# Turning the first two tiles by plain products with the identity in place of transposes, with two more filler products between them

## Chip, cores, metric

One core of one Trainium2 chip. The metric is device time in microseconds of one execution of the program, on its slowest (here its only) core; lower is better.

PE is TensorE, the matrix engine, PEld its loads of weights (in the products with `w1`, the pieces of `w1` are the weights), ACT ScalarE, DVE VectorE, POOL GpSimd, and SPq the queue of SyncE, which issues most transfers. PSUM is the memory that PE writes to. To "turn" a 128x128 block is to transpose it; "the head" is the first 15 us or so.

## The reference, cut to what matters

```python
x = A_x                                   # 2048 x 1024, bf16
xn = layernorm(x)
return x + state_space(xn, ...) + dense_mish(xn, w1, b1, w2)
```

The change touches only the beginning: the first 512 rows of `x` must be normalised, turned so that the 1024 features lie on partitions, and multiplied by `w1`. To start before the statistics of tiles 0 and 1 (128 rows each) are known, the kernel turns their raw `x`, multiplies by `w1`, and corrects for mean and deviation afterwards.

## The kernel before

PE first runs "fillers", products of zeros that nobody reads, to keep it busy while data come. The order of PE in the head is this (cuts marked):

```python
def first_transpose(q):
    for k in range(NK):                                   # 8 blocks of 128 x 128
        bank, d = bank_T(q, k), slice(k * P, (k + 1) * P)
        src, b_src = (xx[:, 0, q, d], b_xx[0][q]) if q < 2 else (xn[:, q, d], b_xn[q])
        PE.mm(lambda e, ...: e.transpose(ps16(bank)[:, d], src, ident[:]), ...)

def first_copy(q, queue, k0=0, k1=NK):                    # PSUM -> xr (q < 2) or xnT
    ...
    srcp = ps16(bank).rearrange("p (k t) -> p k t", k=NK)[:, k0:k1, :]
    # ScalarE copy, or VectorE tensor_copy for tile 3

keep_busy(18)                                             # fillers
first_transpose(0)
keep_busy(14)
first_transpose(1)
keep_busy(6)
# then: 257-column products (256 rows of raw x and a column of ones) with the first piece
# of w1, a spreading of the statistics by 8 small products, products with the second,
# third and fourth piece, between them the turns of tiles 2 and 3, ...
```

Later, on GpSimd, the four loads of `x` for block 1 stand between phase tables, and SP loads B by transposing transfers between the pieces of `w1`:

```python
for j in range(NJ):
    phases(j)                         # GpSimd
    if j == 3:
        for q in range(NQ):
            load_x(PO, 1, q)          # block 1's x
...
SP.dma(lambda e, ...: e.dma_start_transpose(BT[:, ci, j, :, :], src[j * P:(j + 1) * P, :]), ...)
```

## Time and profile before

| | before |
|---|---|
| time, first three runs | 620.87 us median (620.79 to 623.14) |
| span of the profiled run | 619.6 us |
| PE busy | 616.1 us, 99% |
| PE at half rate until | about 6.9 us (128-column products and transposes 103 to 107 ns apart, 56 ns after it) |
| PE's wait for the third w1 piece | 0.22 us as the profile counts it (0.38 us from start to start, see below) |
| first product of tiles 2 and 3 (L553) | 15.45 us |

PE is never short of work from 15.45 us on, so the time is that moment plus a constant, as long as nothing makes PE wait later. The lines that show this stand in the prediction.

### The profile page before, as it was taken

The page shows a single profiled execution, that of the slowest core. Times are in us where ns is not written, and L with a number is a line of the kernel's source. Part 1 is how long each engine was busy: PE and PEld are TensorE (multiplying, and loading weights), DVE is VectorE, ACT ScalarE, POOL GpSimd, SP SyncE. Part 2 cuts the span into 40 slices and gives each one's busy share as a digit, 9 for nine tenths or more (in the row PEclk, how much of TensorE's full clock was granted, in tenths as well). Part 3 has the DMA queues.
Part 4 walks back from the last instruction along what each step waited for, and adds up shares of the span by engine and source line. Part 5 has one row for each costly group of instructions (what it writes and reads, how often), then busy time and mean ns, then how long its engine had stood idle before and what let it go on. Part 6 is the DMA issues. An engine that isn't in the chain of part 4 may idle for free.

```text
span 619.6 us, 7424 instructions
## 1 busy us (share of the span) xinstructions
PE 616.1 (99%) x2957; PEld 288.4 (47%) x2957; DVE 467.3 (75%) x698; ACT 247.5 (40%) x161; POOL 53.1 (9%) x57
## 2 busy tenths in 40 slices
PE   9999999999999999999999999999999999999998
PEld 7644444444444444444444444444444444444444
DVE  6989999999467599998147659999624856999603
ACT  4589997441079940000009992000001999000000
POOL 2899100000100000000010000000000000000000
DMA  8999986840454401783054430286203542033001
GB/s 249 252 254 298 225 167 202 206 136 0 146 191 140 135 2 37 204 201 103 17 187 135 158 114 1 96 184 189 75 35 107 173 162 68 1 123 116 1 0 69
DMA packets 97917, 79.94 MB, mean 129 GB/s; under 512 B 51034, under 2 KB 80346, under 8 KB 97882
## 3 DMA queue, kind: packets, MB, share of 16 engines
q1 hardware_dynamic: 94384, 72.17, 42.3%
q10 hardware_dynamic: 2538, 4.14, 1.8%
q0 software_dynamic: 960, 3.15, 1.8%
q8 instruction: 24, 0.39, 0.3%
q14 instruction: 11, 0.09, 0.1%
HBM read 63.19 MB, written 4.19 MB: 109 GB/s over the span
## 4 chain that ended last, share of the span: by engine, by line
PE 98%; DMA 1%; SPq 1%; issue 0%; DVE 0%
PE ps L820 49%; PE ps L740 29%; PE ps L762 18%; DMA ring<-in_B_w_dram 1%; PE ps L553 1%; PE ps L544 0%; SPq L310 0%; PE ps L834 0%; PE ps L397 0%; SPq L343 0%; SPq L314 0%; DVE xx L888 0%
## 5 line engine op out<-in xcount | busy, mean ns | idle before, releaser
L820 PE MATMUL ps<-ring,act 128*128 128x512 bf16 x896 | 194.0, 379 | 0.0
L740 PE MATMUL ps<-xnT,ring 128*128 128x512 bf16 x840 | 182.0, 379 | 0.0
L718 ACT ACTIVATE act<-hb 128x3584 bf16<-128x3584 bf16 x16 | 50.9, 3183 | 220.6 <-DVE hb L749 220.4
L820 PEld LDWEIGHTS ps<-ring,act 128*128 128x128 bf16 x896 | 87.7, 98 | 105.7
L740 PEld LDWEIGHTS ps<-xnT,ring 128*128 128x128 bf16 x840 | 82.2, 98 | 98.9
L749 DVE TENSOR_SCALAR hb<-ps,par 128x512 bf16<-128x512 f32 (+1 forms) x112 | 80.0, 730 | 52.6 <-PE ps L740 51.7
L762 PE MATMUL ps<-xnT,BT 128*128 128x512 bf16 x512 | 111.2, 379 | 0.0
L820 PE MATMUL ps<-CT,hT 128*128 128x512 bf16 x506 | 109.9, 379 | 0.0
L767 DVE TENSOR_TENSOR mt<-ps,tab 128x1024 bf16<-128x1024 f32 x64 | 75.4, 1219 | 13.3 <-PE ps L762 11.7
L762 PEld LDWEIGHTS ps<-xnT,BT 128*128 128x128 bf16 x512 | 50.1, 98 | 60.4
L820 PEld LDWEIGHTS ps<-CT,hT 128*128 128x128 bf16 x506 | 49.5, 98 | 59.7
L785 DVE TENSOR_TENSOR_SCAN hT<-cs,qi,hT 128x512 bf16<-128x512 f32 x48 | 58.9, 1269 | 0.0
L865 DVE TENSOR_TENSOR xx<-ps,xx 128x1024 bf16<-128x1024 f32 (+1 forms) x16 | 18.8, 1190 | 45.1 <-PE ps L820 45.0
L720 ACT ACTIVATE act<-act 128x3584 bf16<-128x3584 bf16 x16 | 51.0, 3190 | 0.2
L719 ACT ACTIVATE act<-act 128x3584 bf16<-128x3584 bf16 x16 | 51.0, 3190 | 0.2
L790 DVE TENSOR_TENSOR mt<-hT,tab 128x1024 bf16<-128x1024 bf16 x64 | 41.4, 688 | 1.1
L725 DVE TENSOR_TENSOR act<-act,hb 128x3584 bf16<-128x3584 bf16 x16 | 33.2, 2075 | 2.3 <-ACT act L720 2.3
L310 POOL DMA_DIRECT2D xx<-in_A_x_dram x12 | 6.7, 560 | 249.4 <-DVE xx L865 245.1
L694 ACT ACTIVATE ct<-CT,cs 128x512 f32<-128x512 bf16 x16 | 11.5, 718 | 25.3 <-DVE CT L696 25.3
L719 ACT ACT_TABLE_LOAD x16 | 20.5, 1283 | 0.3
L720 ACT ACT_TABLE_LOAD x16 | 20.5, 1283 | 0.3
L785 DVE TENSOR_TENSOR_SCAN hT<-cs,hT 128x512 bf16<-128x512 f32 x16 | 18.7, 1208 | 0.0
(101 smaller groups left out, 294.1 us busy)
## 6 DMA issues: line engine op xcount, KB each, us to landing
ring<-in_B_w_dram SPq DMA_DIRECT2D x112, 512.0 KB, 4.0
out_dram<-xx ACTq DMA_DIRECT2D x15, 256.0 KB, 2.1
xx<-in_A_x_dram POOLq DMA_DIRECT2D x12, 256.0 KB, 4.3
xx<-in_A_x_dram SPq DMA_DIRECT2D x3, 256.0 KB, 4.4
xx<-in_A_x_dram SPq DMA_DIRECT2D x2, 128.0 KB, 2.3
dsk<-in_A_Dskip_dram SPq DMA_DIRECT2D x1, 256.0 KB, 7.4
xnT<-xn SPq DMA_TRANSPOSE x14, 4.6
BT<-in_A_B_re_dram SPq DMA_TRANSPOSE x8, 6.3
```

The lines of the kernel that those rows point to most:

```text
L718: aop(lambda e: e.activation(a, hs, AF.Exp), reads=[b_hb[g % 2]], writes=[b_act[g]])
L719: aop(lambda e: e.activation(a, a, AF.Ln, bias=1.0), reads=[b_act[g]], writes=[b_act[g]])
L720: aop(lambda e: e.activation(a, a, AF.Tanh), reads=[b_act[g]], writes=[b_act[g]])
L725: vop(lambda e: e.tensor_tensor(a, a, hs, op=ALU.mult), reads=[b_act[g], b_hb[g % 2]], writes=[b_act[g]])
L740: PE.mm(lambda e, k=k, w=w: e.matmul(ps[:, bank, :], lhsT=w, rhs=xnT[:, k, :], start=k == 0, stop=k == NK - 1), reads=[b_ring[s]] + b_xnT, ...
L749: vop(lambda e: e.tensor_scalar(hb[:, hs, ts], ps[:, bank, ts], b1(f), None, op0=ALU.add), reads=[b_ps[bank], b_par], writes=[b_hbf[hs]])
L762: PE.mm(lambda e, j=j, ci=ci, k=k, bank=bank: e.matmul(ps[:, bank + ci, :], lhsT=BT[:, ci, j, k, :], rhs=xnT[:, k, :], start=k == 0, stop= ...
L767: vop(lambda e, s=s, u=u, j=j: e.tensor_tensor(mt[:, s, :, :], u, tab[:, s, j, :].unsqueeze(1).to_broadcast([P, 2, TB]), op=ALU.mult), rea ...
L785: vop(lambda e, ci=ci, init=init: e.tensor_tensor_scan(out=hT[:, ci, j, :], data0=cj("r", j).to_broadcast([P, TB]), data1=hT[:, ci, j, :], ...
L790: vop(lambda e, s=s: e.tensor_tensor(mt[:, s, :, :], hT[:, :, j, :], tab[:, s, j, :].unsqueeze(1).to_broadcast([P, 2, TB]), op=ALU.mult), ...
L820: PE.mm(lambda e: e.matmul(ps[:, u, :], lhsT=lhsT, rhs=rhs, start=st_, stop=last), reads=reads, writes=[b_ps[u]], first=st_, last=last)
L865: vop(lambda e: e.tensor_tensor(xr, src, xr, op=ALU.add), reads=b_ps[bank:bank + n] + [b_x], writes=[b_x])
```

## The change

Intent: an earlier or surer full rate of PE. The change rests on an assumption of the author that transposes count less than products towards it; the trace of before didn't show it, and e1, g2 and g3 below refute it (full rate at 5.4, 5.0 and 4.6 us after transposes alone). A product with the identity gives the same turned block, but into fp32 PSUM, half a tile to a bank (128x512 f32). Two more fillers are added between the turns.

```diff
         for k in range(NK):
             bank, d = bank_T(q, k), slice(k * P, (k + 1) * P)
             ...
-            PE.mm(lambda e, ...: e.transpose(ps16(bank)[:, d], src, ident[:]),
+            o = (k % (NK // 2)) * P
+            put = (lambda e, ...: e.matmul(
+                ps[:, bank, o:o + P], lhsT=src, rhs=ident[:], start=True, stop=True)) if q < 2 else (
+                lambda e, ...: e.transpose(ps16(bank)[:, d], src, ident[:]))
+            PE.mm(put, ...
...
-        srcp = ps16(bank).rearrange("p (k t) -> p k t", k=NK)[:, k0:k1, :]
+        srcp = (ps[:, bank, :].rearrange("p (k t) -> p k t", k=NK // 2) if q < 2 else
+                ps16(bank).rearrange("p (k t) -> p k t", k=NK)[:, k0:k1, :])
...
     first_transpose(0)
-    keep_busy(14)
+    keep_busy(16)
     first_transpose(1)
```

In the changed file the lines are five lower: L506 becomes L511, L544 L549, L553 L558, L740 L745, L762 L767; the turns at L397 become L399 (products) and L401 (transposes of tiles 2 and 3).

More of the change, by code (lines that the diff above doesn't have):

```diff
@@ L396, in first_transpose @@
             src, b_src = (xx[:, 0, q, d], b_xx[0][q]) if q < 2 else (xn[:, q, d], b_xn[q])
-            PE.mm(lambda e, bank=bank, d=d, src=src: e.transpose(ps16(bank)[:, d], src, ident[:]),
-                  reads=[b_src.parts[k // (NK // 2)], b_ident], writes=[b_ps[bank]],
+            o = (k % (NK // 2)) * P
+            put = (lambda e, bank=bank, o=o, src=src: e.matmul(
+                ps[:, bank, o:o + P], lhsT=src, rhs=ident[:], start=True, stop=True)) if q < 2 else (
+                lambda e, bank=bank, d=d, src=src: e.transpose(ps16(bank)[:, d], src, ident[:]))
+            PE.mm(put, reads=[b_src.parts[k // (NK // 2)], b_ident], writes=[b_ps[bank]],
                   first=k == 0 or bank != bank_T(q, k - 1), last=k == NK - 1 or bank != bank_T(q, k + 1))
```

## The prediction

Passages that rested on what no trace of this case shows are cut from the prediction, with the cuts marked. The forecast's sum came to 0.0 us for an ordinary run, within 0.1 either way: cost 0.0 at an unchanged clock, gain 0.0 at an earlier one. The steps from "Then sixteen fillers" on suppose one. The 620.3 to 621.7 us rest on the rivals.

> **What bounds the kernel now.** I began with the page: PE is busy 616.1 of 619.6 us, so only time in which PE stands still, or repeats work at a lower clock, can be won. Then I read the chain that ended last in order of time, to see whether the edited part, the first 7 us, is on it (start us, length us, what):
>
> ```profile
> 4.24 7.49 DMA ring<-in_B_w_dram
> 11.73 0.05 issue
> 11.78 1.07 PE ps L544 x8
> 12.84 0.45 PE ps L397 x8
> ...
> 616.14 1.32 PE ps L834 x12
> 617.46 0.02 issue
> 617.49 0.42 DVE xx L888
> ```
>
> From 11.78 us to the end the chain is PE work without a gap (the cut lines are all PE). Before it stands one transfer, the third piece of w1, issued at 4.24 and landed at 11.73; ahead of that are only the SP queue's issues. None of the turning at 3 to 6.5 us is on the chain. The waits of PE in the first 40 us say the same (waited for: us, times, longest):
>
> ```profile
> PE ps L506 <- DVE filler L353: 1.0, 1, 1.0
> PE ps L544 <- DMA ring<-in_B_w_dram: 0.2, 1, 0.2
> ```
>
> PE is idle for 0.22 us before 11.78, because of that transfer. So the head has 0.22 us to spare: what makes it earlier only lengthens this wait, and what makes it later by less than that costs nothing.
>
> Next I read PE's row by row order in the head, for the clock (start, busy, instructions):
>
> ```profile
> 1.04 2.10 PE L506 MATMUL ps<-filler 128*128 128x128 bf16 x18 [1.04 <-DVE filler L353]
> 3.20 1.03 PE L397 MATMUL ps<-ident,xx 128*128 128x128 bf16 x8
> 4.03 1.70 PE L506 MATMUL ps<-filler 128*128 128x128 bf16 x14
> 5.52 1.06 PE L397 MATMUL ps<-ident,xx 128*128 128x128 bf16 x8
> 6.37 0.82 PE L506 MATMUL ps<-filler 128*128 128x128 bf16 x6
> 7.01 1.97 PE L544 MATMUL ps<-xr,ring 128*128 128x257 bf16 x16
> 9.59 1.96 PE L544 MATMUL ps<-xr,ring 128*128 128x257 bf16 x16
> 11.78 1.07 PE L544 MATMUL ps<-xr,ring 128*128 128x257 bf16 x8 [0.22 <-DMA ring<-in_B_w_dram]
> 12.68 0.61 PE L397 MATMUL ps<-ident,xn 128*128 128x128 bf16 x8
> ```
>
> A row holds the spacing of its instructions plus the length of the last one. With the lengths of the groups below (314 ns cold, 219 warm): fillers (2.10-0.31)/17 = 105 ns and (1.70-0.31)/13 = 107 ns; turns (1.03-0.31)/7 = 103 and (1.06-0.31)/7 = 107 ns; the later turns of tile 2 (0.61-0.22)/7 = 56 ns. The 257-column products at 7.01 are (1.97-0.27)/15 = 113 ns apart, as those at 11.78 are ((1.07-0.27)/7 = 114). So PE runs at half rate until about 7.0 us, six microseconds after its first filler, and at full rate after. The column of granted clock says 1.00 throughout and doesn't show this; the durations do:
>
> ```profile
> L506 PE MATMUL ps<-filler 128*128 128x128 bf16 x38 | 4.6, 313 | 1.0 <-DVE filler L353 1.0
> L407 ACT COPY xr<-ps 128x512 bf16<-128x512 bf16 x4 | 2.1, 589 | 0.9 <-PE ps L397 0.9
> L397 PE MATMUL ps<-ident,xx 128*128 128x128 bf16 x16 | 2.1, 312 | 0.1
> L397 PE MATMUL ps<-ident,xn 128*128 128x128 bf16 x16 | 1.2, 219 | 0.0
> L435 ACT COPY yz<-ps 128x512 f32<-128x512 f32 x1 | 0.6, 585 | 0.4 <-PE ps L431 0.4
> ```
>
> [...]the trace shows filler products and transposes at the same 103 to 107 ns, so nothing is lost on PE.[...] The copies agree: 589 ns from bf16 PSUM, 585 ns from fp32.
>
> **The change part by part.** Sixteen transposes become sixteen plain products of the same shape: 16 x about 105 ns before and after at the same clock, difference 0.[...] The banks stay (6 and 4 for tile 0, 7 and 5 for tile 1), half a tile per bank, so no new bank dependence. Four ScalarE copies now read fp32: 4 x (585-589) ns, nothing. Two more fillers: 2 x 106 = 0.21 us if cold, 2 x 56 = 0.11 us if warm.
>
> At an unchanged clock all that follows tile 1's turn shifts by 0.21 us. The first sixteen products then run from 7.22 to about 9.0; the eight spreading products, which started at 9.04 after GpSimd's split (8.30+0.30 = 8.60), start about 0.1 to 0.2 later; the next sixteen end at 11.7 instead of 11.56 (11.78-0.22). The transfer lands at 11.73. Cost: 0.0 us.
>
> [...]Then sixteen fillers take 0.9 us in place of fourteen in 1.5, tile 1 is turned at about 5.0 (its data must have landed) in 0.45 in place of 0.85, six fillers take 0.34, and the sixteen products can start at about 6.0, one microsecond sooner. The spreading still needs the split: GpSimd waited 5.1 us for VectorE's rr, and VectorE's statistics run back to back from 5.03 to 6.5 whatever PE does; at best rr comes 0.1 us sooner. So PE stands still for about a microsecond before the spreading, the second sixteen start at about 9.5, end at about 11.45, and the wait for the transfer is 0.3 us in place of 0.22. Gain: 0.0 us. The transfers can't come sooner: SP issues all nine from 0.79 to 5.25 without waiting for an engine, and the transposing transfers after them hang on VectorE's xn at 7.5, not on PE.
>
> Sum for an ordinary run: 0.0 us, within 0.1 either way.
>
> [...]
>
> **The rivals.** (1) An earlier clock shortens the run, by up to the 0.85+1.7+0.6 us that the cold head wastes. For it: half rate until 7 us. Against: the wait for the transfer at 11.73, with no PE work before it on the chain. It would need an earlier landing; then 619 to 620 us. (2) The extra fillers, or slower fp32 reads, push PE past 11.73: 0.22 us of slack against 0.21, and 585 against 589 ns; at worst 621.0.[...] (4) The 623-us runs come from late transfers and not from the clock; then they stay, and a median of three can land on one.
>
> **Range and chances.** The ordinary run gives 620.8. Below, only rival 1 leads, and the transfer stands against it: 620.3. Above are rivals 2 and 4[...]: 621.7. A change of 2% would be 12.4 us, more than the whole head lasts before the transfer lands, so nothing here reaches it.
>
> **What would show it.** Right: the chain after still begins with the transfer of w1 landing near 11.7 and PE L544 straight after; PE's wait for it is 0.1 to 0.5 us; the turns of tile 1 are 56 ns apart with lengths of about 219 (the clock came early) or[...] still 107; the copies stay at 585 to 590 ns; the spread of runs is narrower. Wrong: the chain leads back through PE or ScalarE before 11.7, the transfer lands at another time, or the products at 9.6 are more than 114 ns apart.

## The result and the profile after

Ratios are the mean time of one kernel's fast runs over that of the other's of the same rounds, so not quite the ratio of the medians. In the first comparison the change took 621.13 us (median of 6, 620.27 to 623.69) and before 621.46 (6 runs, 620.79 to 623.14): ratio 0.9994, interval 0.9970 to 1.0017. In a second comparison (f4 below) it took 621.96 against 620.53, ratio 1.0020, interval 0.9995 to 1.0045. No difference is shown in either direction, and both kernels scatter by some 4 us.

The profiled run of the change was its slowest, 623.69 us (span 622.4), so I read it for what is common to all runs first. PE in the head, in order of time (start, busy, instructions):

```profile
3.20 1.03 PE L399 MATMUL ps<-ident,xx 128*128 128x128 bf16 x8
4.02 1.91 PE L511 MATMUL ps<-filler 128*128 128x128 bf16 x16
5.73 1.06 PE L399 MATMUL ps<-ident,xx 128*128 128x128 bf16 x8
6.58 0.68 PE L511 MATMUL ps<-filler 128*128 128x128 bf16 x6
7.13 1.95 PE L549 MATMUL ps<-xr,ring 128*128 128x257 bf16 x16
10.31 3.17 PE L549 MATMUL ps<-xr,ring 128*128 128x257 bf16 x24 [0.55 <-DMA ring<-in_B_w_dram]
```

The turns take 1.03 and 1.06 us as products, exactly what they took as transposes in before. The fillers' row grew from 1.70 to 1.91 us, the predicted 0.21. The clock is no earlier: the last half-rate product starts at 6.8 us. ScalarE's copies of the turned halves cost what they did, 589 ns from fp32 as from bf16 in before (group: busy, mean ns):

```profile
L412 ACT CAST xr<-ps 128x512 bf16<-128x512 f32 x4 | 2.2, 589 | 1.2 <-PE ps L399 1.2
```

What is new in this run is outside the edited lines. PE's longest wait over the whole span (us in total, times, longest), and the two rows of VectorE that explain it:

```profile
PE ps L767 <- DVE hb L754: 1.8, 1, 1.8
...
```

```profile
47.41 1.43 DVE L449 BATCH_NORM_STATS2 stats<-xx 128x6 f32<-128x512 bf16 x2 [2.51 <-DMA xx<-in_A_x_dram]
...
51.12 1.42 DVE L449 BATCH_NORM_STATS2 stats<-xx 128x6 f32<-128x512 bf16 x2 [0.78 <-DMA xx<-in_A_x_dram]
```

VectorE stood waiting for block 1's `x` until 47.41 us (45.72 in the trace of before) and again until 51.12. The work behind it in program order, the emptying of PSUM banks (L754), came late, and PE stood still for 1.8 us near 62 us, waiting for VectorE. In the head, PE waited for the second piece of w1, until 10.31, and then for the third. The third is missing from PE's list of waits: of the 0.41 us between the starts of the two products, where 0.11 is normal, the first counts as busy for 0.27, and the 0.14 left are too short for that list. The loads of weights show both waits:

```profile
10.30 1.68 PEld L549 LDWEIGHTS ps<-xr,ring 128*128 128x128 bf16 x16 [0.72 <-DMA ring<-in_B_w_dram]
12.40 0.79 PEld L549 LDWEIGHTS ps<-xr,ring 128*128 128x128 bf16 x8 [0.42 <-DMA ring<-in_B_w_dram]
```

So this run is slow by late transfers.

### Where the time goes in every trace

The traces of all fourteen profiled runs add up the same way. "Half rate until" is the start of the last product or transpose with a half-rate duration (the change to full rate after it is called the release below); then come the landing of the third piece of w1, the start of the first product that reads it, and that of the first product of tiles 2 and 3. "Stands still after" sums the gaps between starts of PE's products after that, less the normal spacing (gaps of twice the spacing that recur every 10.8 us are taken for missing records and left out).

| trace | what it is | half rate until | third piece lands | product on it | tiles 2, 3 at | stands still after | run, us |
|---|---|---|---|---|---|---|---|
| before | | 6.9 | 11.73 | 11.78 | 15.45 | 0 | 620.88 |
| after | the change | 6.8 | 12.36 | 12.41 | 16.11 | 2.1 | 623.69 |
| e1 | all turns and fillers transposes | 5.4 | 11.72 | 11.77 | 15.44 | 0 | 620.88 |
| g2 | as e1 | 5.0 | 11.27 | 11.32 | 15.07 | 0.45 | 620.98 |
| g3 | as e1 | 4.6 | 12.08 | 12.12 | 15.85 | 0.46 | 621.76 |
| e2 | the change, 14 fillers | 6.7 | 11.40 | 11.45 | 15.20 | 0.9 | 621.60 |
| e3 | before, 26 fillers | 6.9 | 11.53 | 12.25 | 15.88 | 2.1 | 623.31 |
| e4 | the change, block 1's x early | 6.4 | 11.42 | 11.47 | 15.22 | 0 | 620.57 |
| f1 | before, no fillers | 12.0 | 11.84 | 13.98 | 17.61 | 0 | 622.97 |
| f2 | before, block 1's x early | 6.3 | 12.63 | 12.67 | 16.40 | 2.3 | 624.17 |
| f3 | as e4 | 5.7 | 12.01 | 12.06 | 15.76 | 0 | 621.11 |
| f4 | the change | 5.6 | 12.18 | 12.22 | 15.95 | 2.1 | 623.42 |
| g1 | the change, B loaded plainly | 6.0 | 12.02 | 12.07 | 15.75 | 0 | 621.10 |
| h1 | the change | 4.1 | 11.77 | 11.82 | 15.50 | 1.9 | 622.74 |

Take "tiles 2, 3 at" and "stands still after" from the span, and 604.1 us remain in each, within 0.1. (The time of a run is some 1.3 us over its span.) The edit could act directly only on the head, where single runs of one kernel differ by 0.6 us (h1 and after).

What sets the head is in the table too. In twelve of the fourteen traces the product on the third piece starts 0.05 us after that piece lands, and tiles 2 and 3 follow 3.67 to 3.76 us later, whether full rate came at 4.1 or at 6.9 us. (With fillers it came from 3.1 us, in h1 and g3, to 5.9 us, in before, after PE's first instruction, which starts at 1.04 us, in g3 at 1.50.) Only in e3 and f1, whose heads were made late or slow on purpose, had the piece been there before PE was ready for it.

### The profile page after: what moved, and what is told of

It is laid out like the page before. It is cut to its first block, busy times and chain, and to the rows that moved or that the text cites. A ratio compares the mean times of both kernels' runs of the same rounds, so it can differ in the third digit from the quotient of the medians.

```text
span 622.4 us, 7428 instructions
## 1 busy us (share of the span) xinstructions
PE 616.7 (99%) x2959; PEld 288.3 (46%) x2959; DVE 468.1 (75%) x698; ACT 248.1 (40%) x161; POOL 54.5 (9%) x57
## 4 chain that ended last, share of the span: by engine, by line
PE 90%; POOL 4%; DMA 2%; DVE 2%; issue 1%; SPq 0%; POOLq 0%; DVEq 0%
PE ps L825 49%; PE ps L745 23%; PE ps L767 18%; DMA xx<-in_A_x_dram 2%; POOL py L627 1%; POOL px L625 1%; POOL ph_h L629 1%; DVE stats L449 1%; POOL rb L568 1%; DVE hb L754 1%; DVE act L730 0%; PE ps L839 0%; DVE stats L371 0%; SPq L310 0%; SPq L343 0%
## 5 line engine op out<-in xcount | busy, mean ns | idle before, releaser
L745 PE MATMUL ps<-xnT,ring 128*128 128x512 bf16 x840 | 182.1, 379 | 0.0
L745 PEld LDWEIGHTS ps<-xnT,ring 128*128 128x128 bf16 x840 | 82.1, 98 | 99.2 <-DVE hb L754 0.7
L754 DVE TENSOR_SCALAR hb<-ps,par 128x512 bf16<-128x512 f32 (+1 forms) x112 | 80.0, 730 | 52.6 <-PE ps L745 51.7
L767 PE MATMUL ps<-xnT,BT 128*128 128x512 bf16 x512 | 111.3, 379 | 1.8 <-DVE hb L754 1.8
L772 DVE TENSOR_TENSOR mt<-ps,tab 128x1024 bf16<-128x1024 f32 x64 | 75.4, 1219 | 13.3 <-PE ps L767 11.7
L767 PEld LDWEIGHTS ps<-xnT,BT 128*128 128x128 bf16 x512 | 50.0, 98 | 62.5 <-DVE hb L754 2.3
L449 DVE BATCH_NORM_STATS2 stats<-xx 128x6 f32<-128x512 bf16 x24 | 16.3, 679 | 3.7 <-DMA xx<-in_A_x_dram 3.3
```

Of the source, the lines that this page charges most:

```text
L449: vop(lambda e, h=h: e.bn_stats(stats[:, s, h, :], xx[:, i, q, h * 512:(h + 1) * 512]), reads=[b_xx[i][q]], writes=[b_stats[s]])
L745: PE.mm(lambda e, k=k, w=w: e.matmul(ps[:, bank, :], lhsT=w, rhs=xnT[:, k, :], start=k == 0, stop=k == NK - 1), reads=[b_ring[s]] + b_xnT, ...
L754: vop(lambda e: e.tensor_scalar(hb[:, hs, ts], ps[:, bank, ts], b1(f), None, op0=ALU.add), reads=[b_ps[bank], b_par], writes=[b_hbf[hs]])
L767: PE.mm(lambda e, j=j, ci=ci, k=k, bank=bank: e.matmul(ps[:, bank + ci, :], lhsT=BT[:, ci, j, k, :], rhs=xnT[:, k, :], start=k == 0, stop= ...
L772: vop(lambda e, s=s, u=u, j=j: e.tensor_tensor(mt[:, s, :, :], u, tab[:, s, j, :].unsqueeze(1).to_broadcast([P, 2, TB]), op=ALU.mult), rea ...
```

## The experiments

Times of full rate that the expectations drew from a figure which no trace shows are cut and marked. What is left at half rate is estimated from the trace of before: 257-column products are taken to be 257/128 x 107 = 215 ns apart, so that sixteen take 3.4 us.

### e1: every filler a transpose too

```diff
-  e.matmul(ps[:, 3, 0:P], lhsT=filler[:], rhs=filler[:], start=True, stop=True)
+  e.transpose(ps16(3)[:, 0:P], filler[:], ident[:])
-keep_busy(18)
+keep_busy(16)
```

> The kernel before, with its 38 fillers made transposes too (16+14+6; the first two dropped because they now wait for the identity, ready at about 1.36 us). The first products are then the 257-column ones at about 7.0 us. If transposes don't count for the clock: [...]the first sixteen products take about 3.4 us in place of 1.97, the product after the third w1 piece starts at about 12.9 instead of 11.78, and the time is 1.0 to 1.3 us longer than before. Rival, transposes count as products do: full rate at about 6.9 us as in both traces so far, first sixteen products 113 ns apart, time within 0.2 us of before.

Measured: 621.43 us against 620.94, ratio 0.9997 (0.9974 to 1.0020). PE in the head:

```profile
1.50 1.86 PE L506 MATMUL ps<-ident,filler 128*128 128x128 bf16 x16 [1.50 <-POOL kon L359]
3.16 1.06 PE L397 MATMUL ps<-ident,xx 128*128 128x128 bf16 x8
4.01 1.69 PE L506 MATMUL ps<-ident,filler 128*128 128x128 bf16 x14
5.51 0.64 PE L397 MATMUL ps<-ident,xx 128*128 128x128 bf16 x8
5.98 0.50 PE L506 MATMUL ps<-ident,filler 128*128 128x128 bf16 x6
6.69 1.95 PE L544 MATMUL ps<-xr,ring 128*128 128x257 bf16 x16 [0.21 <-ACT xr L407]
```

The second turn takes 0.64 us in place of 1.06: its transposes and the fillers behind them are 56 ns apart ((0.50-0.22)/5), full rate. Until then PE had done nothing but transposes since the kernel began. So full rate came, from about 5.4 us, after transposes alone, and transposes run at it themselves (56 ns apart in place of 107). The theory that the change is built on falls, so far on one trace.

### g2 and g3: e1's kernel twice more, one look each

> The kernel of e1 again, for a second trace of when the clock comes. If transposes count as products do: full rate[...] before any product has run long.[...]

> The kernel of e1 once more, a third trace of when the clock comes. If transposes count as products do: full rate[...]. If not:[...] after the first product.

Measured: half rate until 5.0 and 4.6 us; 620.98 and 621.76 us. Three of three heads of transposes alone were released before any product. g3's 4.6 is 3.1 us after its first filler, e1's 5.4 is 3.9; why g3's came so early is open. They are even earlier than most heads with products (4.1 to 6.9 us), but with three traces, and h1 at 4.1, I make nothing of that.

### f1: no fillers at all

The three calls of `keep_busy` are taken out of the kernel before.

> The kernel before without any filler; PE does only the two turns by transposes until the first 257-column products. e1 showed full rate at 5.45 us after nothing but transposes. If PE's activity, of whichever kind, releases the clock: with the head mostly idle (two turns of about 0.85 us between 3.2 and 6.4 us) [...]the first sixteen 257-column products are up to 215 ns apart (3 us or more in place of 1.95) and the time is 0 to 1 us longer than before. Rival, the release is a matter of time since the start and not of activity: full rate again between 5.4 and 7.0 us and no loss.

Measured: 622.03 us against 620.53, ratio 1.0016 (0.9994 to 1.0038). By that interval the time decides nothing, though all six runs are at 621.45 or above and ten of the eleven of before at 621.16 or below. The trace decides. Its head:

```profile
5.03 1.03 PE L397 MATMUL ps<-ident,xx 128*128 128x128 bf16 x8 [0.83 <-DMA xx<-in_A_x_dram]
7.50 3.62 PE L541 MATMUL ps<-xr,ring 128*128 128x257 bf16 x16 [1.44 <-DMA ring<-in_B_w_dram]
...
12.04 2.99 PE L541 MATMUL ps<-xr,ring 128*128 128x257 bf16 x24
```

The sixteen products take 3.62 us in place of 1.95, 213 ns apart ((3.62-0.42)/15; the trace gives them a mean length of 420 ns), and full rate comes only after the product at 12.04 us, although the third piece of w1 had landed at 11.84. Tiles 2 and 3 start at 17.61, over a microsecond later than in any trace with fillers. So the release does follow PE's activity (12.0 us without fillers, 4.1 to 6.9 with them), and fillers earn their place; which kind of instruction fills made no difference that these traces show.

### e2: the change with 14 fillers

```diff
-    keep_busy(16)
+    keep_busy(14)
```

> The change without its two extra fillers. My theory, the third piece of w1 rules: time as before within the scatter of transfers (620.3 to 623.7), full rate again at about 6.9 us[...], turn of tile 1 at 5.5 us. Rival, the two fillers are what cancelled a gain of the products: 0.2 us or more faster than the change.

Measured: 621.05 us against 620.94, ratio 0.9990 (0.9965 to 1.0015); the second turn at 5.49 us, half rate until 6.7. In this run PE's list shows no wait for a transfer in the head, and tiles 2 and 3 started at 15.20. So no gain of 0.2 us that the two fillers hide was seen, though the scatter is wider than that. Nor is their cost: e4, with 16 fillers and no listed wait either, began the 257-column products 0.11 us later (7.12 for 7.01) and tiles 2 and 3 at 15.22, because both heads ended on the third piece (11.40 and 11.42).

### e3: 26 fillers before the second turn

```diff
-    keep_busy(14)
+    keep_busy(26)
```

> The kernel before with 12 more fillers between the turns (26 in place of 14). Tests the slack of 0.22 us. If PE has only that much to spare: the first 257-column product starts at about 7.7 to 7.9 in place of 7.0, PE no longer waits for the third w1 piece (0.2 us before), and the time is 0.4 to 0.9 us longer than before. Rival, the head has more slack than the wait shows: time within 0.2 us of before.

Measured: 621.12 us against 620.94, ratio 1.0000 (0.9973 to 1.0027). The trace has the late head that I expected (first 257-column product at 7.99 us, no wait for a piece of w1, tiles 2 and 3 at 15.88): the third piece had landed at 11.53, and PE came to it 0.7 us later, at 12.25. The time doesn't show the 0.4 to 0.9 us, but its interval, some 1.7 us either way, can't exclude them: two of six runs were near 623 and one at 620.18. An earlier release shortens these fillers to half (56 ns apart in place of 107, as h1 shows), which would make the cost vary from run to run; that was not seen in e3's trace. How much slack a run has hangs on when its third piece lands, 11.27 to 12.63 us in the fourteen traces, so 0.22 us is no constant of the kernel.

### e4, f3, f2: block 1's x earlier

In the change (e4, f3: one kernel, twice) and in before (f2):

```diff
-        if j == 3:
+        if j == 1:
             for q in range(NQ):
                 load_x(PO, 1, q)
```

> The change, with block 1's four loads of x issued by GpSimd after two phase tables instead of four (near 31 us instead of 42). Theory: runs near 623 are those in which these loads land late (first statistics waited to 47.4 in the slow trace of the change, to 45.7 in the trace of before) so that PE stands still 1.8 us near 62. Then in this kernel VectorE's wait for these loads is gone, PE has no wait near 62 us and no run is above 622. Rival, the slow runs come from the head's transfers: about one run in four stays near 623.

> The kernel of e4 unchanged, to see whether its 627.0 of six runs comes back. If the early loads take away the main cause of the runs near 623: at least five of six at 620.2 to 621.2, mean 0.3 to 0.8 us under that of before. If not: runs near 623 in two or three of six, as before.

> The kernel before (transposes, 14 fillers) with block 1's x loads issued after two phase tables, as in e4. If those loads cause the slow runs and the turning is immaterial: VectorE doesn't wait for them, PE has no gap over 0.3 us between 14 us and the end, five or six of six runs lie at 620.2 to 621.0, and it equals e4. If products matter beside that: e4's kernel is 0.3 us or more faster than this one.

Measured: e4 620.63 us against 620.94, ratio 1.0002 (0.9966 to 1.0038), five of six runs at 620.37 to 620.92 and one at 627.0. f3, the same kernel: 622.85 against 620.53, ratio 1.0032 (1.0000 to 1.0065), with 624.60, 625.58 and 625.90 among six. f2: 622.19 against 620.53, ratio 1.0021 (0.9996 to 1.0046). VectorE no longer waits for block 1's `x` in any of these traces, but PE's waits in f2 are:

```profile
PE ps L740 <- DMA ring<-in_B_w_dram: 1.9, 1, 1.9
PE ps L544 <- DMA ring<-in_B_w_dram: 1.1, 1, 1.1
```

My theory that these loads make the slow runs fell as a remedy: with them moved earlier, f2's trace has a piece of w1 late instead. It is no improvement. The runs at 624.6 to 627 left no trace, so what was late in them is open. Late transfers may not be all: of the seven runs above 624.5, here and among those of before and f4, five have a mean granted clock of 0.997, and every other run whose clock is on record has 1.000. A clock lower by 0.3% over 620 us would be 1.9 us (an estimate from these two numbers). What lowered it was not looked for.

### g1: B loaded plainly

```diff
-  e.dma_start_transpose(BT[:, ci, j, :, :], src[j * P:(j + 1) * P, :])
+  e.dma_start(BT[:, ci, j, :, :].rearrange("p k d -> p (k d)"), src[j * P:(j + 1) * P, :])
```

> The changed kernel with the sixteen transposing loads of B (SP, between 16 and 52 us) made plain loads of the same bytes. The result is wrong on purpose. If these transposing loads delay block 1's x and the w1 pieces behind them, and that is the scatter: VectorE's wait for x near 45 us is under 0.5 us, PE has no wait between 17 and 65 us and six of six runs lie within 1 us of the lowest. If the scatter comes from transfers in general or from elsewhere: one or two of six still lie 2 us or more above the lowest.

Measured: wrong result; 620.91 us, all five runs between 620.62 and 621.10, against 621.02 (ten runs, one at 624.17); ratio 1.0000 (0.9986 to 1.0013). VectorE doesn't wait for block 1's `x`, and PE has no wait after 17 us. The SP queue shows what changed. The first row is from h1, an ordinary transposing load of B; the second from g1 (start, time the queue was held):

```profile
45.02 5.97 SPq L710 DMA_TRANSPOSE BT<-in_A_B_re_dram  x1
```

```profile
45.51 1.28 SPq L710 DMA_DIRECT2D BT<-in_A_B_im_dram  x1
```

These are the longest in the two traces. In the traces of before, after and h1 a transposing load of B held the queue for 1.2 to 6.0 us (longest in h1), in g1 a plain one of the same 256 KB for 0.42 to 1.28. Times to landing don't differ like this (medians 5.9 and 6.5 us in h1, 6.1 and 6.6 in g1). In the ten traces with transposing loads in which block 1's `x` is loaded as in before, VectorE waits 1.0 to 4.2 us for it, in g1 not at all. This supports the transposing loads of B as what makes the later transfers late, but five runs without a slow one are few, when 8 of the 39 runs of before were above 622; and whether it is the held queue or the transfer itself was not separated.

### f4 and h1: the change again

> The changed kernel unchanged, for six more runs and a second trace. My theory (transposes count for the clock and the head is mostly hidden): same as before within 0.3 us in the mean, runs scattered over 620.2 to 623.7, full rate between 5.4 and 7.0 us. Rival, the change narrows the scatter: no run above 621.5.

> The changed kernel once more, for a trace of it in an ordinary run, since both its traces so far fell on runs above 623. If the time is head plus stalls: PE's first product of tiles 2 and 3 starts at 15.2 to 15.8 us, the rest takes 604.1 us plus whatever PE stands still between 20 and 65 us, so 620.5 to 621.2 without such a stall. If the change itself costs or gains in the head: that product starts outside 15.1 to 16.0 with no transfer awaited.

Measured: f4 as told above, runs from 620.83 to 624.90, so the change doesn't narrow the scatter (5 of its 13 runs are above 622, against 8 of 39 of before, too few to tell whether it widens it); half rate until 5.6 us, PE standing still 2.1 us between 49 and 62 us. h1: 622.74 us, one run beside one of before at 620.79. h1 is the most telling trace of the change, because here the clock came early. PE:

```profile
4.02 1.21 PE L511 MATMUL ps<-filler 128*128 128x128 bf16 x16
5.07 0.61 PE L399 MATMUL ps<-ident,xx 128*128 128x128 bf16 x8
5.52 0.50 PE L511 MATMUL ps<-filler 128*128 128x128 bf16 x6
7.47 1.96 PE L549 MATMUL ps<-xr,ring 128*128 128x257 bf16 x16 [1.45 <-DMA ring<-in_B_w_dram]
```

Its longest wait, and the load of weights from the third piece:

```profile
PE ps L745 <- DMA ring<-in_B_w_dram: 1.7, 1, 1.7
```

```profile
11.81 0.78 PEld L549 LDWEIGHTS ps<-xr,ring 128*128 128x128 bf16 x8 [0.20 <-DMA ring<-in_B_w_dram]
```

Everything that an earlier clock can give is there: fillers in 1.21 us in place of 1.91, the second turn in 0.61 in place of 1.06. PE then stood still for 1.45 us for the first piece of w1 and began the 257-column products at 7.47, later than in before (7.01). After that gap they are 113 ns apart ((1.96-0.27)/15), still full rate. Even after so late a start PE was in time for the third piece, which landed at 11.77: without the wait for the first piece it would have waited longer for the third. And 15.50 + 604.1 + 1.9 = 621.5 is its span.

## Why the prediction was right, and where it was not

Measured 621.13 us for 620.8, inside 620.3 to 621.7, and no change of 2%. That the number fell inside is in part luck: with runs from 620.3 to 624.9, the second six (f4) have a median of 621.96, outside. By its own steps:

- **The swap costs nothing: right.** Turns 1.03 and 1.06 us before and after, at full rate 0.61 us as transposes (g2) and as products (h1); copies 589 ns before and after.
- **The fillers cost 0.21 us, hidden: right.** Their row grew by 0.21 us, and in every trace of a head with 16 fillers (after, e4, f3, f4, g1, h1) PE was in time for the third piece.
- **The head hangs on the third piece of w1: right as a mechanism.** It holds in twelve of fourteen traces, all seven with products for turns among them. The moment is not fixed at 11.73: the piece landed from 11.27 to 12.63. The slack was read too small: a product's 273 ns overlap the next, so from start to start PE lost 0.50-0.11 = 0.38 us before 11.78 (unrounded 495 and 113 ns), not 0.22. The sign "the chain begins with the transfer near 11.7" failed in the profile of the change because of the stall near 62 us: there the chain leads back through VectorE, block 1's `x` and GpSimd.
- **With an earlier clock the first sixteen products start at about 6.0: wrong.** The first piece of w1, which they read, landed at 6.44 us in before and at 6.42 to 7.70 in the fourteen traces; the prediction left it out. That PE would then stand still before the spreading wasn't seen; its "second sixteen at about 9.5" agrees with the landing of the second piece, 9.54 in before, and not for the reason given.
- **An earlier clock gains nothing: right.** h1 shows it, where PE waits for the first piece and still meets the third as it lands, and so do g3 and g2: full rate from 4.6 and 5.0 us, and the third piece at 12.08 and 11.27 us ended both heads. After the wait of 1.45 us in h1 the products were still 113 ns apart.
- **The premise, that transposes count less for the clock: wrong.** This is the step that failed. It was not shown by the trace of before. With fillers and turns all products the release was at 4.1 to 6.8 us, with transposes for the turns at 6.3 to 6.9, and e1, g2 and g3 were released by transposes alone, at 5.4, 5.0 and 4.6.
- **The spread of runs is narrower: not seen.** The change ran from 620.27 to 623.69 us against 620.79 to 623.14 of before, and in the second comparison from 620.83 to 624.90 against 620.25 to 624.71. The reason given, that slow runs come from a late clock and would go, was not shown. Rival 4, late transfers, is what the traces of 623-us runs show: PE standing still 2.1 us after the head in the change and in e3. For the runs above 624.5 the cause stays open.

So the change did nothing because its premise is false, and would have done nothing in the ordinary run if it had been true, because the landing of the third piece ends the head. A difference between 0.3% faster and 0.4% slower is not excluded (0.9970 to 1.0017, and 0.9995 to 1.0045): the scatter hides it.

## What to carry to other kernels

Before changing instructions to please a clock, run a head that holds nothing but the suspected kind: three traces of transposes alone (full rate from 5.4, 5.0 and 4.6 us) answered what the mixed head of before could not. Where PE is 99% busy, split the span into the moment when the work becomes continuous plus the gaps after it; here that sum held in fourteen traces, and showed that most of the scatter lay in gaps at 49 to 62 us (0 to 2.3 us), far from the edited lines, and the rest in the landing of w1 (tiles 2 and 3 at 15.07 to 16.40 with fillers). A slack read from one run isn't the kernel's slack: look at when the last transfer landed in several runs, and measure PE's gaps from start to start.
